# A sorted attention with a squared-ReLU feed-forward: batch 1's keys two positions per product, and the work around them reordered

## The chip, the cores and the metric

The kernel runs on one core of one Trainium2 chip. Its time is the device time of one execution in microseconds (us), a median over runs. The engines are named as in the profile: PE (TensorE: matrix products, with PEld for its weight loads), DVE (VectorE), ACT (ScalarE), POOL (GpSimd, which also issues the loads that convert fp32 to bf16) and SP (SyncE, which issues the other transfers). A name with a q behind it (SPq) is an engine's queue issuing or waiting.

## What is computed

```python
# q, k, v: (4, 8, 768, 64) fp32; sort_net: (4, 8, 8, 8); blocks of 96 positions
P = sort_net
for _ in range(5):                       # softmax-like normalisation of rows, then columns
    P = exp(P - max(P, -1)); P = P / (sum(P, -1) + 1e-9); P = P / (sum(P, -2) + 1e-9)
k_sorted = einsum('bhij,bhjcd->bhicd', P, k_blocks)      # mixes the 8 blocks
v_sorted = einsum('bhij,bhjcd->bhicd', P, v_blocks)
attn = softmax(q_block @ k_sorted_block.T / 8)            # inside each block
x = (attn @ v_sorted_block) as (3072 tokens, 512)
out = (s * relu(x @ w_in)**2 + b) @ w_out                 # w_in 512 x 2048, w_out 2048 x 512
```

## The kernel before

There are 4 batches, and each gives two token tiles of 384 tokens; tile t = 2b + half, t = 0 to 7. A token tile goes through `ffn1(t)` (16 chunks of the hidden dimension, two at a time: four products of 384 columns for each chunk, L474, then ReLU on ACT, L486, and the square on DVE, L487) and `ffn2(t)` (three groups m of 128 tokens, 16 accumulating products of 512 columns each, L498, then `store`: one DVE step, L519, that adds the bias and writes the tile `ot`, and one transfer, L522). For the last tile, `ffn2` treats its last group in parts of columns (L511).

The order on every engine is the order of the program text. The attention of the next batch is done inside the feed-forward of the present one: `ffn1` and `ffn2` take a dictionary `slots`, and call the closures of a slot between their own products. In `ffn2`, slot m*4 + f//4 follows the product f = 3, 7, 11 or 15 of group m; slot 3 thus comes at the end of group 0, behind its `store`. `halves(n)` makes the slots for batch n: `s0` for `ffn2(2(n-1))`, `s1` for `ffn2(2(n-1)+1)`.

What the closures do:

- `K` / `k_piece` (L294): sorts the keys of 16 positions with 32 products of 64 columns into one PSUM tile `tp` and moves it to `KS` with one instruction. `KP` / `k_pairs` (L304): the same with 8 products of 128 columns, two positions each, into `tpp`; four moves, two by each of DVE (L206) and ACT (L204). Before the change, batch 1 uses `K` and batches 2 and 3 use `KP`.
- `V` / `v_piece` (L330): sorts values from `VP` (a permuted copy of the values, made by ACT and POOL) into `VS`. Only batches 0 and 1 use it. For batches 2 and 3, `v_rows` (L349) sorts the values in place and `v_back` sends them through memory (`vd`) to `VS` by SP transfers.
- `SC` / `s_piece` (L381): scores of one head pair and half of the blocks; ACT then takes the exponential (L389). `P` / `p_piece` (L423): products with the values; DVE divides (L428, L429) into `x`. `TD` / `t_dma`: SP's transposing transfer of `x` into `xt`, which `ffn1` reads.
- `PDB` / `build_pd`: five small DVE steps that build the sorting matrix `PD` of a batch.
- `make_bias`: column sums of `w_out` on PE (L573), four DVE steps (L575, L578), and three POOL copies (L581) that spread the result over 128 partitions. `store` reads it.
- `load_q_rows` (L116): eight loads on POOL of one block of queries each, into `qtok`; `q_dma` (L457): two transposing transfers on SP, one for each half of the blocks, into `qt`.

PSUM is in two pools: `psa` with three buffers of two banks (tag "a": `hps`, `tp`, `tpp`, `tv`, `sc`, `pv`, `cps`, in turn), and `psb` with two buffers of one bank (tag "b": `ops` and others). A buffer is written again only when its last reader is done. `ot` has three buffers, which come free when their transfer has landed.

On POOL, batch 1's loads come in this order: values, keys, queries; then the copies of `make_bias`; then `after` (a wait for the end of `ffn1(1)`) and `v_sort` (the second part of `VP`); then batch 2's value loads, which wait for the second query transpose (L90). On SP, the two query transposes come before all stores.

Of the kernel before, what the change touches and what calls it, by code (L numbers as in the profile page):

```python
# [9 lines left out]
FP = mybir.dt.float32  # L10
BF = mybir.dt.bfloat16
# [11 lines left out]
def kernel(  # L23
# [12 lines left out]
    nc = tc.nc  # L36

    B, H, S, D = q.shape
    NB = sort_net.shape[-1]
    BLK = S // NB  # L40
    BH = B * H
    NHP = H // 2
    d_model = H * D
    d_ff = moe_w_in.shape[1]
    NF = d_ff // 128
    HB = NB // 2
    TG = HB * BLK
# [5 lines left out]
    CK = 16  # L53
# [6 lines left out]
    rawp = ctx.enter_context(tc.tile_pool(name="rawp", bufs=2))  # L60
# [9 lines left out]
    psb = ctx.enter_context(tc.tile_pool(name="psb", bufs=2, space=bass.MemoryType.PSUM))  # L70
# [9 lines left out]
    for c in range(0, C2, CV):  # L80
        nc.sync.dma_start(out=v0f[:, c:c + CV, :].rearrange("p c d -> p (c d)"),
                          in_=raw[2][0][:, c * D:(c + CV) * D])

    RAW = {}

    def load(t, b, parts=1, behind=None):
        ti = rawp.tile([128, C2, D], BF, tag=f"raw{t}", name=f"raw{t}")
        RAW[t, b] = ti
        if behind is not None:
            nc.gpsimd.tensor_copy(out=ti[0:behind.shape[0], 0, 0:1], in_=behind)  # L90
        n = C2 // parts
        for c in range(0, C2, n):
            nc.gpsimd.dma_start(out=ti[:, c:c + n, :].rearrange("p c d -> p (c d)"),  # L93
                                in_=raw["qkv".index(t)][b][:, c * D:(c + n) * D])
# [12 lines left out]

    QTOK = {}

    def load_q_rows(b):  # L110

        ti = rawp.tile([BLK, NB, H, D], BF, tag="rawq", name="qtok")
        qv = q[b].rearrange("h (n t) d -> t n h d", n=NB)
        for n in range(0, NB, 2):
            for h in range(2):
                nc.gpsimd.dma_start(out=ti[:, n + h], in_=qv[:, n + h])  # L116
        QTOK[b] = ti

    zeros = const.tile([128, 512], BF)
    nc.vector.memset(zeros, 0.0)  # L120
# [58 lines left out]
    for t, src in ((s_bc, moe_s), (b_bc, moe_b)):  # L179
        nc.gpsimd.dma_start(out=t, in_=src.to_broadcast([128, 1]))  # L180
    load("k", 1, 6)
    load_q_rows(1)

    rstat = const.tile([BH, NB], FP)
    rrec = const.tile([BH, NB], FP)
# [16 lines left out]
    def evac(eng, out, in_):  # L202
        if eng == "A":
            nc.scalar.copy(out=out, in_=in_)  # L204
        else:
            nc.vector.tensor_copy(out=out, in_=in_)  # L206

    def q_banks(b, half, engs):
# [3 lines left out]
        for u in range(2):  # L212
# [13 lines left out]
            out=jsel, in_=ident.rearrange("p (h j z) -> p j h z", h=H, j=NB), axis=AX.XY, op=ALU.add),  # L226
        lambda: nc.vector.tensor_reduce(
            out=bm.rearrange("p (e z a) -> p e z a", e=2, z=2),
            in_=idv.rearrange("p a e j z -> p e z a j"), axis=AX.X, op=ALU.add),
# [67 lines left out]
                                 start=True, stop=True)  # L297
        evac(eng, KS[b % 2][:, :, :, c0:c0 + CK], ps.rearrange("p c z g -> p g z c"))

    def k_pairs(b, c0):  # L300
        m = CK // 2
        ps = psa.tile([128, m, 2, 2 * NG], FP, tag="a", name="tpp")
        for j in range(m):
            nc.tensor.matmul(out=ps[:, j].rearrange("p e g -> p (e g)"),  # L304
                             lhsT=RAW["k", b][:, c0 + 2 * j:c0 + 2 * j + 2, :].rearrange(
                                 "p c d -> p (c d)"),
                             rhs=PD[b].rearrange("p e z g -> p (e z g)"), start=True, stop=True)
        for e in range(2):
            for u in range(2):
                evac("DA"[e],  # L310
                     KS[b % 2][e * 64:(e + 1) * 64, :, :, c0 + u:c0 + CK:2],
                     ps[u * 64:(u + 1) * 64, :, e].rearrange("p c (z g) -> p g z c", z=2))

# [38 lines left out]

    def v_back(b):
        vd = drp.tile([2, 2, NG, C2, D], BF, tag="vd", name="vd")
        nc.sync.dma_start(out=vd.rearrange("e z g c d -> (e z g) (c d)"),
                          in_=RAW["v", b].rearrange("p c d -> p (c d)"))
        for z in range(2):
            for e in range(2):
                nc.sync.dma_start(
                    out=VS[b % 2][z * GAP:z * GAP + C2, e * NG:(e + 1) * NG, 0:D],  # L360
                    in_=vd[e, z].rearrange("g c d -> c g d"))
# [116 lines left out]
    def ffn1(t, slots, done={}):  # L478

        gt = gtp.tile([128, NF, TG], BF, tag="gt", name="gt")  # L480
        GT[t] = gt
        for i in range(NF // 2):
            part(t, i, range(done.get(i, 0), NHP))
            rt = rtp.tile([128, 2, TG], BF, tag="rt", name="rt")
            h = H1.pop((t, i))[:, :, 0:TG]
            nc.scalar.activation(out=rt, in_=h, func=AF.Relu)  # L486
            nc.vector.tensor_tensor(out=gt[:, 2 * i:2 * i + 2, :], in0=rt, in1=rt, op=ALU.mult)  # L487
            for p in slots.get(i, ()):
                p()
        XT.pop(t)  # L490

    def ffn2(t, slots):
        gt = GT.pop(t)
        last = t == 2 * B - 1
        for m in range(TG // 128 - int(last)):
            ops = psb.tile([128, d_model], FP, tag="b", name="ops")
            for f in range(NF):
                nc.tensor.matmul(out=ops, lhsT=gt[:, f, m * 128:(m + 1) * 128],  # L498
                                 rhs=wo[:, f, :], start=(f == 0), stop=(f == NF - 1))
                if f % 4 == 3:  # L500
                    if f == NF - 1:
                        store(t, m, ops)
                    for p in slots.get(m * 4 + f // 4, ()):
                        p()
        if last:
            m = TG // 128 - 1
            for n0 in range(0, d_model, d_model // 2):
                ns = slice(n0, n0 + d_model // 2)
                ops = psb.tile([128, d_model // 2], FP, tag="b", name="ops")
                for f in range(NF):  # L510
                    nc.tensor.matmul(out=ops, lhsT=gt[:, f, m * 128:(m + 1) * 128],  # L511
                                     rhs=wo[:, f, ns], start=(f == 0), stop=(f == NF - 1))
                store(t, m, ops, ns)
# [3 lines left out]
    def store(t, m, ops, ns=slice(0, d_model)):  # L517
        ot = osb.tile([128, d_model], FP, tag="ot", name="ot")
        nc.vector.scalar_tensor_tensor(out=ot[:, ns], in0=ops, scalar=s_bc, in1=BIAS[0][:, ns],  # L519
                                       op0=ALU.mult, op1=ALU.add)  # L520
        r0 = t * TG + m * 128
        nc.sync.dma_start(out=out[r0:r0 + 128, ns], in_=ot[:, ns])  # L522
# [46 lines left out]
    def make_bias():  # L569
        cps = psa.tile([128, d_model], FP, tag="a", name="cps")  # L570
        for f in range(NF):
            r = slice(f % 4 * 32, f % 4 * 32 + 32)
            nc.tensor.matmul(out=cps[r], lhsT=ones, rhs=wo[:, f, :],  # L573
                             start=(f < 4), stop=(f >= NF - 4), tile_position=(0, f % 4 * 32))
        nc.vector.tensor_scalar(out=bias[0:32], in0=cps[0:32], scalar1=b_bc[0:32], scalar2=None,  # L575
                                op0=ALU.mult)
        for r in range(32, 128, 32):
            nc.vector.scalar_tensor_tensor(out=bias[0:32], in0=cps[r:r + 32], scalar=b_bc[r:r + 32],  # L578
                                           in1=bias[0:32], op0=ALU.mult, op1=ALU.add)
        for r in range(32, 128, 32):  # L580
            nc.gpsimd.tensor_copy(out=bias[r:r + 32], in_=bias[0:32])  # L581

    def QF0(): return lambda: q_banks(0, 1, "AD")
    def SB(i): return lambda: s_banks(0, 1, i)
    def K(b, i, eng): return lambda: k_piece(b, i * CK, eng)
    def KP(b, i): return lambda: k_pairs(b, i * CK)
    def V(b, i, eng): return lambda: v_piece(b, i * CK, eng)
    def SC(b, h, i): return lambda: s_piece(b, h, i)
    def P(b, h, i): return lambda: p_piece(b, h, i)
    def TP(b, h, i, eng): return lambda: t_piece(b, h, i, eng)  # L590
    def VRW(b, u): return lambda: v_rows(b, u)
    def VB(b): return lambda: v_back(b)
    def TD(b, h): return lambda: t_dma(b, h)
    def PDB(b): return lambda: build_pd(b, later[:, b % 2, b // 2, :])
# [4 lines left out]
    def halves(n):  # L599

        if n == 1:
            s0 = {4: [K(n, 0, "D"), K(n, 1, "A"), K(n, 2, "D")],
                  8: [V(n, 0, "D"), V(n, 1, "A"), V(n, 2, "D")],
                  10: [V(n, 3, "A")]}
        else:
            s0 = {0: [KP(n, 0), KP(n, 1), KP(n, 2)]}
        s1 = {0: [SC(n, 0, 0), SC(n, 0, 1)],
              3: [P(n, 0, 0), SC(n, 0, 2), SC(n, 0, 3)], 4: [P(n, 0, 1)], 5: [P(n, 0, 2)],
              6: [P(n, 0, 3), TD(n, 0), SC(n, 1, 0), SC(n, 1, 1)], 8: [P(n, 1, 0)],
              9: [P(n, 1, 1), SC(n, 1, 2), SC(n, 1, 3)], 10: [P(n, 1, 2)],  # L610
              11: [P(n, 1, 3), TD(n, 1)]}
        return s0, s1

    ffn1(0, {0: [QF0()], 2: [SB(0)], 3: [P(0, 1, 0), SB(1)], 4: [P(0, 1, 1), SB(2)],
# [5 lines left out]
    part(1, 1, (0, 1))  # L620
    part(1, 0, (2,))
    part(1, 1, (2,))
    ffn1(1, {2: [PDB(1)], 4: [make_bias], 6: [PDB(2)], 7: [PDB(3)]}, {0: 3, 1: 3})
    q_dma(1)
    for d in (0, CK):
        permute(nc.scalar, 1, RAW["v", 1], ds=slice(d, d + CK))
# [3 lines left out]
    s0, s1 = halves(1)  # L630
    ffn2(0, s0)
    ffn2(1, s1)
    for b in range(1, B):
        n = b + 1
        s0, s1, u0, u1 = {}, {}, {}, {}
        if n < B:
            load("k", n, 6, XT[2 * b + 1][:, HB - 1, NHP - 1, 0:1])
            load_q_rows(n)
            s0, s1 = halves(n)
# [38 lines left out]
```

## Time and profile before

| | |
|---|---|
| median of 3 runs | 223.43 us (222.94 to 223.51) |
| profiled execution: time, span | 223.59 us, 221.8 us |
| PE, DVE, ACT, POOL busy | 214.8, 123.3, 106.1, 70.6 us |
| granted PE clock | 1.00 |
| first-stage products L474 | 512, 87.9 us busy |
| second-stage products L498 | 350 recorded, 82.4 us busy |
| moves of the keys: `tp`, DVE / ACT | 1216 ns / 1012 ns each |
| moves of the keys: `tpp`, DVE / ACT | 728 ns / 725 ns each |
| output transfers, 256 KB / 128 KB | 2.5 us / 1.7 us to landing (median) |

The span runs from the first to the last instruction; the execution's time holds some more around it. The chain of waits follows the work back from the last instruction, at each step to what released it; a line of it gives the start, the length and what ran. Some matmul records are missing from a trace, which shows as a count that is too low and a small gap called "issue". A group's line gives the line number, the engine, the operation, out<-in, the shape and the count, then the busy time and mean of one, then the idle time of the engine just before.

### The profile page before, as it was taken

The page shows a single profiled execution, that of the slowest core. Times are in us where ns is not written, and L with a number is a line of the kernel's source. Part 1 is how long each engine was busy: PE and PEld are TensorE (multiplying, and loading weights), DVE is VectorE, ACT ScalarE, POOL GpSimd, SP SyncE. Part 2 cuts the span into 40 slices and gives each one's busy share as a digit, 9 for nine tenths or more (in the row PEclk, how much of TensorE's full clock was granted, in tenths as well). Part 3 has the DMA queues.
Part 4 walks back from the last instruction along what each step waited for, and adds up shares of the span by engine and source line. Part 5 has one row for each costly group of instructions (what it writes and reads, how often), then busy time and mean ns, then how long its engine had stood idle before and what let it go on. Part 6 is the DMA issues. An engine that isn't in the chain of part 4 may idle for free.

```text
span 221.8 us, 5257 instructions
## 1 busy us (share of the span) xinstructions
PE 214.8 (97%) x2212; PEld 129.6 (58%) x2231; DVE 123.3 (56%) x251; ACT 106.1 (48%) x144; POOL 70.6 (32%) x127
## 2 busy tenths in 40 slices
PE   7999999999999999999999999999999999999993
PEld 5977766555655555666446555655446556654453
DVE  6767457549754767546616677548417744442121
ACT  4677687656144344664622535665424355650000
POOL 7659791669914004930032008800000000000000
PEclk9999999999999999999999999999999999999999
DMA  6999999999999632999999546999911440001212
GB/s 154 280 165 126 125 162 207 204 177 117 116 182 165 183 96 46 138 236 127 91 252 171 138 121 91 236 147 92 221 69 50 121 120 0 0 3 47 95 47 95
DMA packets 66935, 28.92 MB, mean 130 GB/s; under 512 B 51808, under 2 KB 62816, under 8 KB 66912
## 3 DMA queue, kind: packets, MB, share of 16 engines
q0 software_dynamic: 31168, 12.85, 49.6%
q1 hardware_dynamic: 35744, 15.74, 34.3%
q8 instruction: 17, 0.28, 0.6%
q14 instruction: 6, 0.05, 0.1%
HBM read 28.85 MB, written 7.86 MB: 165 GB/s over the span
## 4 chain that ended last, share of the span: by engine, by line
PE 95%; DVE 2%; issue 1%; ACT 0%
PE hps L474 38%; PE ops L498 36%; PE z L132 5%; PE pv L423 4%; PE sc L381 3%; PE ops L511 2%; PE tv L330 2%; PE tp L294 1%; PE tpp L304 1%; PE tvr L349 1%; DVE vs L206 1%; PE tr L440 1%; PE scb L399 1%; PE sc L259 0%; PE pv L417 0%
## 5 line engine op out<-in xcount | busy, mean ns | idle before, releaser
L474 PE MATMUL hps<-xt,wi 128*128 128x384 bf16 x512 | 87.9, 326 | 0.0
L498 PE MATMUL ops<-wo,gt 128*128 128x512 bf16 x350 | 82.4, 379 | 1.5 <-issue 0.8
L486 ACT ACTIVATE rt<-hps 128x768 bf16<-128x768 f32 x64 | 51.8, 811 | 39.5 <-PE hps L474 38.8
L474 PEld LDWEIGHTS <-wi 128*128 128x128 bf16 x512 | 49.0, 98 | 32.6 <-issue 0.4
L487 DVE TENSOR_TENSOR gt<-rt 128x768 bf16<-128x768 bf16 x64 | 35.6, 558 | 41.2 <-ACT rt L486 41.0
L498 PEld LDWEIGHTS <-gt 128*128 128x128 bf16 x368 | 34.0, 98 | 37.2
L519 DVE SCALAR_TENSOR_TENSOR ot<-ops,s_bc,bias 128x512 f32<-128x512 f32 (+1 forms) x25 | 18.2, 729 | 37.9 <-PE ops L498 34.4
L389 ACT ACTIVATE at<-sc 112x768 bf16<-112x768 f32 x24 | 18.1, 808 | 31.8 <-PE sc L381 31.8
L429 DVE TENSOR_TENSOR x<-pv,rec 96x512 bf16<-96x512 f32 x32 | 22.0, 687 | 1.1
L116 POOL DMA_DIRECT2D qtok<-in_q_dram x24 | 18.6, 810 | 0.7 <-DMA rawk<-in_k_dram 0.6
L423 PEld LDWEIGHTS <-at 112*128 112x128 bf16 (+1 forms) x256 | 12.9, 101 | 6.7 <-ACT at L389 1.0
L142 POOL DMA_DIRECT2D wi<-in_moe_w_in_dram x24 | 13.0, 583 | 6.0 <-DMA qh<-in_q_dram 3.1
L423 PE MATMUL pv<-vs,at 112*128 112x66 bf16 (+1 forms) x256 | 13.9, 195 | 0.1
L93 POOL DMA_DIRECT2D rawk<-in_k_dram x21 | 11.2, 551 | 4.3 <-DMA rawv<-in_v_dram 2.0
L132 PE MATMUL z<-zeros 128*64 128x96 bf16 (+2 forms) x129 | 10.8, 257 | 1.3 <-DVE zeros L120 1.2
L93 POOL DMA_DIRECT2D rawv<-in_v_dram x18 | 9.7, 555 | 5.5 <-DMA wo<-in_moe_w_out_dram 4.7
L204 ACT CAST ks<-tpp 64x512 bf16<-64x512 f32 x12 | 8.7, 725 | 4.4 <-DVE ks L206 4.1
L132 PEld LDWEIGHTS <-zeros 128*64 128x64 bf16 (+1 forms) x130 | 8.5, 128 | 3.0 <-DVE zeros L120 1.2
L90 POOL COPY rawk<-xt 128x1 bf16<-128x1 bf16 x2 | 0.4, 190 | 31.1 <-DMA xt<-x 31.1
L428 DVE RECIPROCAL rec<-pv 96x8 f32<-96x8 f32 x32 | 6.4, 200 | 6.4 <-PE pv L423 6.4
L206 DVE CAST ks<-tpp 64x512 bf16<-64x512 f32 x12 | 8.7, 728 | 0.2
L351 DVE CAST rawv<-tvr 128x512 bf16<-128x512 f32 x12 | 8.2, 683 | 0.0
(93 smaller groups left out, 141.6 us busy)
## 6 DMA issues: line engine op xcount, KB each, us to landing
out_dram<-ot SPq DMA_DIRECT2D x23, 256.0 KB, 2.5
rawv<-in_v_dram POOLq DMA_DIRECT2D x18, 128.0 KB, 5.1
rawk<-in_k_dram POOLq DMA_DIRECT2D x18, 128.0 KB, 4.5
qtok<-in_q_dram POOLq DMA_DIRECT2D x24, 96.0 KB, 6.7
wo<-in_moe_w_out_dram POOLq DMA_DIRECT2D x4, 512.0 KB, 10.4
v0f<-in_v_dram SPq DMA_DIRECT2D x4, 384.0 KB, 7.1
vd<-rawv SPq DMA_DIRECT2D x2, 768.0 KB, 6.8
vs<-vd SPq DMA_DIRECT2D x8, 192.0 KB, 7.4
```

The lines of the kernel that those rows point to most:

```text
L93: nc.gpsimd.dma_start(out=ti[:, c:c + n, :].rearrange("p c d -> p (c d)"), in_=raw["qkv".index(t)][b][:, c * D:(c + n) * D])
L116: nc.gpsimd.dma_start(out=ti[:, n + h], in_=qv[:, n + h])
L132: nc.tensor.matmul(out=z[0:m, 0:w], lhsT=zeros[:, 0:m], rhs=zeros[:, 0:w], start=True, stop=True)
L142: nc.gpsimd.dma_start(out=wi[:, al, f0:f1], in_=wiv[:, al, f0:f1])
L389: nc.scalar.activation(out=at, in_=sc[0:KR, :, 0:TG], func=AF.Exp, scale=scale)
L423: nc.tensor.matmul(out=pv[0:m, e, n * VW:(n + 1) * VW], lhsT=atf[:, c0:c0 + m], rhs=VS[b % 2][:, e * NG + g0 + n, :], start=True, stop=True)
L429: nc.vector.tensor_tensor(out=x[:, :, hp * 128:(hp + 1) * 128].rearrange("p n (e d) -> p e n d", e=2), in0=pvv[:, :, :, 0:D], in1=rec.unsq ...
L474: nc.tensor.matmul(out=H1[t, i][:, f, 0:TG], lhsT=wi[:, hp, fc:fc + 128], rhs=XT[t][:, :, hp, :], start=(hp == 0), stop=(hp == NHP - 1))
L486: nc.scalar.activation(out=rt, in_=h, func=AF.Relu)
L487: nc.vector.tensor_tensor(out=gt[:, 2 * i:2 * i + 2, :], in0=rt, in1=rt, op=ALU.mult)
L498: nc.tensor.matmul(out=ops, lhsT=gt[:, f, m * 128:(m + 1) * 128], rhs=wo[:, f, :], start=(f == 0), stop=(f == NF - 1))
L519: nc.vector.scalar_tensor_tensor(out=ot[:, ns], in0=ops, scalar=s_bc, in1=BIAS[0][:, ns], op0=ALU.mult, op1=ALU.add)
```

## The change

- Batch 1's keys are sorted by `k_pairs` in slot 3 of `ffn2(0)`, where `k_piece` did it in slot 4. `k_pairs` takes the order of the engines; for batch 1 ACT moves the first half of the partitions and DVE the second, for the others it stays DVE, then ACT.
- Batch 1's values: three tiles in slot 9 (were in slot 8), the fourth in slot 0 of `ffn2(1)` ahead of the scores (was in slot 10 of `ffn2(0)`).
- `load_q_rows` takes the blocks to load, in the same order as before. For batch 1 the last three blocks are loaded at the end of `make_bias`, behind its POOL copies.
- The `PD` of batches 2 and 3 is built in slot 1 of `ffn2(1)` and `ffn2(3)`; it was built in slots 6 and 7 of `ffn1(1)`.
- `v_back` writes `vd` in two halves of 64 partitions, and reads back the first half first.
- In the last token tile, the second group's output is stored in two halves of the columns, and the third group is computed and stored in parts of 256, 128 and 128 columns (were 256 and 256).

```diff
-    def load_q_rows(b):
-        ti = rawp.tile([BLK, NB, H, D], BF, tag="rawq", name="qtok")
+    def load_q_rows(b, ns=range(NB)):
+        if b not in QTOK:
+            QTOK[b] = rawp.tile([BLK, NB, H, D], BF, tag="rawq", name="qtok")
         qv = q[b].rearrange("h (n t) d -> t n h d", n=NB)
-        for n in range(0, NB, 2):
-            for h in range(2):
-                nc.gpsimd.dma_start(out=ti[:, n + h], in_=qv[:, n + h])
-        QTOK[b] = ti
+        for n in ns:
+            nc.gpsimd.dma_start(out=QTOK[b][:, n], in_=qv[:, n])
...
-    load_q_rows(1)
+    load_q_rows(1, range(NB - 3))
...
-    def k_pairs(b, c0):
+    def k_pairs(b, c0, engs):
...
-                evac("DA"[e],
+                evac(engs[e],
...
-        nc.sync.dma_start(out=vd.rearrange("e z g c d -> (e z g) (c d)"),
-                          in_=RAW["v", b].rearrange("p c d -> p (c d)"))
-        for z in range(2):
-            for e in range(2):
+        for e in range(2):
+            nc.sync.dma_start(out=vd[e].rearrange("z g c d -> (z g) (c d)"),
+                              in_=RAW["v", b][e * 64:(e + 1) * 64].rearrange("p c d -> p (c d)"))
+        for e in range(2):
+            for z in range(2):
...
-                    if f == NF - 1:
+                    if f == NF - 1 and last and m == TG // 128 - 2:
+                        for n0 in range(0, d_model, d_model // 2):
+                            ns = slice(n0, n0 + d_model // 2)
+                            store(t, m, ops[:, ns], ns)
+                    elif f == NF - 1:
...
-            for n0 in range(0, d_model, d_model // 2):
-                ns = slice(n0, n0 + d_model // 2)
-                ops = psb.tile([128, d_model // 2], FP, tag="b", name="ops")
+            for n0, w in ((0, 256), (256, 128), (384, 128)):
+                ns = slice(n0, n0 + w)
+                ops = psb.tile([128, w], FP, tag="b", name="ops")
...
         for r in range(32, 128, 32):
             nc.gpsimd.tensor_copy(out=bias[r:r + 32], in_=bias[0:32])
+        load_q_rows(1, range(NB - 3, NB))
...
-            s0 = {4: [K(n, 0, "D"), K(n, 1, "A"), K(n, 2, "D")],
-                  8: [V(n, 0, "D"), V(n, 1, "A"), V(n, 2, "D")],
-                  10: [V(n, 3, "A")]}
+            s0 = {3: [KP(n, 0, "AD"), KP(n, 1, "AD"), KP(n, 2, "AD")],
+                  9: [V(n, 0, "D"), V(n, 1, "A"), V(n, 2, "D")]}
...
+        if n == 1:
+            s1[0] = [V(n, 3, "A")] + s1[0]
+        if n + 1 < B:
+            s1[1] = [PDB(n + 1)]
...
-    ffn1(1, {2: [PDB(1)], 4: [make_bias], 6: [PDB(2)], 7: [PDB(3)]}, {0: 3, 1: 3})
+    ffn1(1, {2: [PDB(1)], 4: [make_bias]}, {0: 3, 1: 3})
```

More of the change, by code (lines that the diff above doesn't have):

```diff
@@ L585, in K, with KP @@
     def K(b, i, eng): return lambda: k_piece(b, i * CK, eng)
-    def KP(b, i): return lambda: k_pairs(b, i * CK)
+    def KP(b, i, engs="DA"): return lambda: k_pairs(b, i * CK, engs)
     def V(b, i, eng): return lambda: v_piece(b, i * CK, eng)
```

## The prediction

> **What bounds the kernel now.** I read the page's busy times first, then the chain of waits in order of time, then the timelines of the engines around the changed places.
>
> ```profile
> PE 214.8 (97%) x2212; PEld 129.6 (58%) x2231; DVE 123.3 (56%) x251; ACT 106.1 (48%) x144; POOL 70.6 (32%) x127
> ```
>
> PE is busy 97% of the span. The chain, cut to the places that the change touches (start, length, what):
>
> ```profile
> 50.53 4.26 PE ops L498 x19
> 54.80 1.64 PE tp L294 x96
> 56.44 0.16 issue
> 56.60 3.40 PE ops L498 x15
> 60.00 1.64 PE tv L330 x96
> ...
> 63.47 0.62 PE tv L330 x32
> 64.09 1.83 PE ops L498 x8
> 65.93 0.45 PE sc L381 x16
> ...
> 102.75 1.34 PE tpp L304 x24
> 104.09 4.96 PE ops L498 x23
> ...
> 214.91 3.51 PE ops L511 x32
> 218.42 0.03 issue
> 218.44 0.48 DVE ot L519
> ```
>
> From 20.9 us on every piece of the chain is PE. Its "issue" gaps are mostly missing records (L498 has 368 weight loads, but 350 matmuls): a `ops` product takes 4.96 / 23 = 0.216 us, and 0.16 + 0.05 is one of them. So PE never waits there. Only two things can shorten the time: fewer PE cycles, or a shorter end behind the last product. Everything else can only cost, by making PE wait.
>
> **The change part by part.** (1) *Batch 1's keys in pairs.* Removed: 96 products of 64 columns. By instruction starts, 50.53 to 59.93 holds 35 `ops` products (7.55 us), the keys, and a gap of 0.095 us before the values: the keys cost 9.39 - 7.55 - 0.095 = 1.75 us (1.64 in the chain, and a like gap before them). Added: 24 products of 128 columns, as batch 2's at 102.75, 1.34 us with no gap on either side. Saving 0.41 us; 0.31 if the gap stays.
>
> A rule speaks against this: the Trainium skill, "TensorE: Matmul & The Clock Gate", section "Back-to-back issue gap", gives about 81 ns for each 128-column product in a stream where each has its own weight load. By that 24 products would take an estimated 1.94 us, 0.2 us more than now, and the 32 products of part (6) 2.6 us instead of 1.75. This trace has just such a stream, L304, at 1.34 / 24 = 56 ns, so the measurement decides.
>
> The price is in the moves out of PSUM (lines L206 and L204, busy and mean ns):
>
> ```profile
> L206 DVE CAST ks<-tpp 64x512 bf16<-64x512 f32 x12 | 8.7, 728 | 0.2
> L206 DVE CAST ks<-tp 128x1024 bf16<-128x1024 f32 x3 | 3.6, 1216 | 0.3 <-PE tp L294 0.3
> ```
>
> Before, DVE had two moves of 1.22 us and ACT one of 1.01; now each has six of 0.73, 4.4 us. In batch 2 the second engine starts on a tile when the first has done both its moves (DVE 103.24 to 107.70, ACT 104.79 to 109.25). Here ACT goes first: its two `vp` copies end at 51.23 + 2.97 = 54.20, the first tile is done at about 54.6, so ACT works 54.6 to 59.1. DVE first has the store of tile 0, now held only by the bias (part 2) to 55.3 + 0.75 = 56.05, then moves to 60.5. The products start at 53.99 (slot 3), after the last key chunk landed at 52.1. The values follow at 53.99 + 1.34 + 24 x 0.216 = 60.5; their third tile needs the third key tile's buffer at 61.6. Slack 1.1 us, so I cost the moves at nothing; each us beyond it would be a us of PE.
>
> (2) *Bias copies ahead of three query loads* on POOL:
>
> ```profile
> 49.50 6.16 POOL L116 DMA_DIRECT2D qtok<-in_q_dram  x8
> 55.65 1.93 POOL L581 COPY bias<-bias 32x512 f32<-32x512 f32 x3
> 57.77 3.24 POOL L198 COPY vp<-rawv 128x384 bf16<-128x384 bf16 x4
> 65.57 0.19 POOL L90 COPY rawv<-qt 128x1 bf16<-128x1 bf16 x1 [4.57 <-DMA qt<-qtok]
> ```
>
> Five loads of 0.77 end at 53.36; DVE's bias sums ended at 52.2; so the copies run 53.36 to 55.29, and the store that waited 1.2 us for them comes 2.3 us sooner. The last three loads end at 57.6 instead of 55.65; the `vp` copies stay at 57.8. Behind the last load (landed 60.89) stands SP's second transpose, and behind that the stores:
>
> ```profile
> 55.46 6.89 SPq L457 DMA_TRANSPOSE qt<-qtok  x2
> 62.40 7.82 SPq L522 DMA_DIRECT2D out_dram<-ot  x4
> ```
>
> The shift is between 0 (the DMA engines were busy throughout, and do the same work) and 1.95 us (the issue's whole delay); I take 1. The first store lands at 66.15 + 1 = 67.1 (68.1 at worst); its `ot` buffer, one of three, is wanted at 68.5: nothing. The second transpose lands at 66.5 (67.5), wanted at about 72.6: nothing. Batch 2's value loads, released by it, land at 74.5 (75.4) instead of 73.5, and now overlap the `xt` transpose at 73.6. That took 3.5 us; the query transpose amid loads took 6.4, the one after them 4.6, so it lands between 77.1 and 79.0, wanted at 79.0. Nothing, at the edge.
>
> (3) *Two `build_pd` moved* out of `ffn1(1)`: 1.25 us of DVE each. They now run after the stores at 65.10 and 113.62, ahead of 3.25 us of idle DVE each. Nothing; without that idle time they would delay `x` and so PE.
>
> (4) *Values at slot 9, the fourth tile with the scores.* PE work is the same. One interruption of the `ops` stream goes: alone the fourth tile costs 0.09 + 0.63 = 0.72 us (32 of the 96 cost 0.55) and the two scores 0.11 + 0.45 = 0.56, together 1.28; in one block 1.09 to 1.17. Bounds: 0 to 0.19 saved; I take 0.15, since the score blocks behind `pv` show no gap. ACT evacuates the tile in 1.02 us ahead of the exponentials, which then end at 67.3 and 68.1; the first `pv` comes at 68.6. Slack 1.3 us.
>
> (5) *`v_back` in halves.* The whole write took 90.77 to 98.18, the reads' issue until 106.9, the first query transpose lands at 112.22, the scores start at 114.38, now 113.8. Halved, the first reads can go at 94.5 to 98.2. Hidden either way: no gain. Bound for the loss: if each half takes the whole 7.41 us, the third read goes at 105.6 instead of 99.6, and PE waits 6.0 - 1.6 = 4.4 us. I take nothing: 768 KB in 7.41 us is 104 GB/s, beside the key and query loads, and two halves hold the same bytes.
>
> The Trainium skill, "SBUF — State Buffer", section "Can I just issue two DMAs to hit both halves?", says that such halves run one after the other, at little over the rate of one. With its 196 GB/s for 64 partitions that is an estimated 4 us for both, so the rule would give no loss here either.
>
> (6) *Last outputs.* The store of tile 1 becomes two of 0.48, done at 215.9 before the next at 216.66. The last tile is 256 + 128 + 128 columns: 32 products at 55.8 for 16 at 109.5 ns, 0.035 us more. The last DVE step shrinks: 512 columns took 0.75, 256 took 0.48, so 128 take 0.35: 0.13 saved. The last transfer: 256 KB took 2.0 us, 128 KB 1.7; 64 KB take 1.55 to 1.7; I take 0.1 saved. Then SP's closing waits. SP's transfers use eight semaphores in turn; before, the last of 52 fell on the fourth, and after its landing at 220.66 four waits of 0.06 us for the others followed. With four more transfers (two in `v_back`, one in each of the split stores) the last falls on the eighth, and those waits are over before it lands: 0.24 saved, or 0 if the order changes.
>
> Sum: 0.41 + 0.15 - 0.035 + 0.13 + 0.1 + 0.24 = 1.0 us. The profiled execution took 223.59 us, 1.79 beyond its span of 221.8, and 0.16 above the median of 223.43. So: span 220.8, profiled 222.6, median 222.4.
>
> **Rivals.** (A) *Only the products count*: the closing waits keep their order, the fourth value tile saves nothing, or the `xt` transpose costs PE about 0.5 us. Then the gain is 0.4 to 0.6: about 222.9. For it: the semaphore order is inferred, and the transpose is at the edge. Against: the eight semaphores do go round without a break in this trace. (B) *Slower: the halved write holds the queries back.* Place: SP's third read of batch 2, at 99.6 us, with the query transposes queued behind it. It decides from the second half landing later than 99.6 + 1.6 = 101.2 us, 10.4 after its issue; at the bound PE waits 4.4 us: 223.43 - 1.0 + 4.4 = 226.8. At half that wait it is 224.6. Against: 104 GB/s beside other loads is no limit of this write alone. (C) *The pairs don't save*: PE waits at slot 9 for the third key tile, because the moves run longer beside POOL's copies. 1.5 us beyond the slack of 1.1 cancels all: 223.4 to 223.9. Against: the 24 moves in batches 2 and 3 all took about 0.73.
>
> **How the numbers follow.** A change of 0.3%, 0.67 us, is about what a measurement of this kernel can tell from none. Forecast 0.67 (222.0 to 222.75), A 0.17, C 0.08, B 0.08. Faster by more than that is the forecast's share, 0.67; A and most of C lie within, 0.24; B and C's worst are slower, 0.09. The range's low end is the sum with every upper value (0.41 + 0.19 - 0.035 + 0.13 + 0.15 + 0.24 = 1.09, 222.3) less 0.3 for the runs' own spread (222.94 to 223.51); its high end takes in A with a small stall, 223.2.
>
> **What would show it.** In the changed profile: `tpp` x24 in 1.34 us near 54 us; no PE idle time before L330, L423 and L474 between 54 and 82 us; the last DVE `ot` at about 0.35 us; the last landing within 0.1 us of SP's last wait; span near 220.8. Wrong: a wait of PE for ks moves near 61 us, for `xt` near 79, or for `qt` near 114.

## The result and the profile after

The changed kernel takes 222.70 us (222.26 to 222.91), the kernel before 223.41 (222.94 to 225.46) beside it: a ratio of 0.9961, 95% interval 0.9950 to 0.9971. By the ratio that is 0.87 us less (0.65 to 1.12); the medians differ by 0.71 us, the means by 0.85. The forecast was 222.4, the range 222.0 to 223.2.

The profiled execution took 222.54 us, its span is 220.4. First the page's busy times and the chain of waits at the same places as before (start, length, what); line numbers have moved by a few, L497 is L498, L302 is L304, L328 is L330, L380 is L381, L514 is L511 and L522 is L519.

```profile
PE 213.6 (97%) x2156; PEld 128.8 (58%) x2175; DVE 126.0 (57%) x257; ACT 109.4 (50%) x149; POOL 70.8 (32%) x127
```

```profile
50.12 3.40 PE ops L497 x15
53.52 1.34 PE tpp L302 x24
54.86 2.16 PE ops L497 x10
57.02 0.05 issue
57.08 2.97 PE ops L497 x13
60.04 1.64 PE tv L328 x96
61.68 0.16 issue
61.84 2.54 PE ops L497 x11
64.38 0.62 PE tv L328 x32
65.00 0.45 PE sc L380 x16
...
213.99 3.55 PE ops L514 x48
217.54 0.03 issue
217.56 0.35 DVE ot L522
```

The keys' 24 products take 1.34 us, 56 ns each, as batch 2's did; the fourth value tile stands directly ahead of the scores; from 53 to 79 us no piece is a wait of PE. The last DVE step is 0.35 us long.

To compare two executions I count from the first product of the bias (line L573 before), because the stage ahead of it, which the change leaves alone, ended at 44.96 to 45.43 us in the profiled executions of this study, whatever the kernel. The two profiled executions differ thus:

| stretch, us | before | after | difference |
|---|---|---|---|
| start to the first bias product | 45.43 | 45.02 | -0.41 (not the change's) |
| to the first `pv` product of batch 1 | 23.477 | 22.967 | -0.510 |
| from there to the last DVE step | 149.536 | 149.580 | +0.044 |
| last DVE step | 0.484 | 0.351 | -0.133 |
| last transfer, issue to landing | 1.706 | 1.555 | -0.151 |
| landing to the end of the span | 1.159 | 0.918 | -0.241 |

Without the first row the sum is -0.99 us; the forecast's sum was -1.0.

Not all of this arrives in the time, which is longer than the span by a part that no trace here shows. For the kernel before, that part was 1.72 to 1.84 us (85 executions beside the experiments, median 1.77); for the changed kernel it was 2.09 to 2.22 (22 executions, median 2.13). So 0.36 us of what the span gained is lost outside it. The part goes with the kernel more than with the execution: about 1.8 us in the kernels below with only the last outputs, with four more transfers, with only the keys in pairs and with DVE first, 2.0 with the sorted values written whole, 1.7 to 2.1 with the fourth tile in pairs, and 2.1 in the others. Its cause stays open. Where it differs between two kernels, their spans tell more than their times; the median span is 220.6 us for the changed kernel and 221.6 to 221.7 for the kernel before.

The three timelines of the changed places (start, length, engine, line, what). POOL:

```profile
48.19 3.87 POOL L115 DMA_DIRECT2D qtok<-in_q_dram  x5
52.04 2.17 POOL L584 COPY bias<-bias 32x512 f32<-32x512 f32 x3
54.17 2.29 POOL L115 DMA_DIRECT2D qtok<-in_q_dram  x3
56.63 3.24 POOL L196 COPY vp<-rawv 128x384 bf16<-128x384 bf16 x4
```

DVE, then ACT:

```profile
54.25 0.75 DVE L522 SCALAR_TENSOR_TENSOR ot<-ops,s_bc,bias 128x512 f32<-128x512 f32 x1 [1.16 <-POOL bias L584]
55.51 4.52 DVE L204 CAST ks<-tpp 64x512 bf16<-64x512 f32 x6 [0.50 <-ACT ks L202]
60.06 0.75 DVE L522 SCALAR_TENSOR_TENSOR ot<-ops,s_bc,bias 128x512 f32<-128x512 f32 x1
60.73 2.34 DVE L204 CAST vs<-tv 112x1024 bf16<-112x1024 f32 x2
```

```profile
54.01 4.53 ACT L202 CAST ks<-tpp 64x512 bf16<-64x512 f32 x6 [0.21 <-PE tpp L302]
```

ACT moves keys from 54.0 to 58.5, DVE a tile behind to 60.03. The third value tile (60.04 + 2/3 of 1.64 = 61.1) finds its buffer free by 1.1 us, as worked out; by the starts of the products it is less, 0.84 us, as the memsets below show.

### The profile page after: what moved, and what is told of

It is laid out like the page before. It is cut to its first block, busy times and chain, and to the rows that moved or that the text cites. A ratio compares the mean times of both kernels' runs of the same rounds, so it can differ in the third digit from the quotient of the medians.

```text
span 220.4 us, 5172 instructions
## 1 busy us (share of the span) xinstructions
PE 213.6 (97%) x2156; PEld 128.8 (58%) x2175; DVE 126.0 (57%) x257; ACT 109.4 (50%) x149; POOL 70.8 (32%) x127
## 4 chain that ended last, share of the span: by engine, by line
PE 90%; DMA 5%; DVE 1%; issue 1%; POOL 1%; ACT 0%; POOLq 0%
PE hps L473 38%; PE ops L497 36%; DMA rawk<-in_k_dram 5%; PE pv L422 4%; PE sc L380 3%; PE tpp L302 2%; PE ops L514 2%; PE tv L328 2%; PE tvr L347 1%; DVE vs L204 1%; PE tr L439 1%; PE scb L398 1%; POOL rawk L93 0%; PE sc L257 0%; PE pv L416 0%
## 5 line engine op out<-in xcount | busy, mean ns | idle before, releaser
L497 PE MATMUL ops<-wo,gt 128*128 128x512 bf16 x350 | 82.4, 379 | 1.4 <-issue 0.6
L497 PEld LDWEIGHTS <-gt 128*128 128x128 bf16 x368 | 34.1, 98 | 37.4
L522 DVE SCALAR_TENSOR_TENSOR ot<-ops,s_bc,bias 128x512 f32<-128x512 f32 (+2 forms) x27 | 18.6, 691 | 34.7 <-PE ops L497 31.6
L202 ACT CAST ks<-tpp 64x512 bf16<-64x512 f32 x18 | 13.2, 731 | 4.7 <-DVE ks L204 4.1
L204 DVE CAST ks<-tpp 64x512 bf16<-64x512 f32 x18 | 13.1, 729 | 0.9 <-ACT ks L202 0.5
L130 PE MATMUL z<-zeros 128*64 128x96 bf16 (+2 forms) x129 | 9.8, 241 | 1.3 <-DVE zeros L118 1.2
L130 PEld LDWEIGHTS <-zeros 128*64 128x64 bf16 (+1 forms) x130 | 7.5, 115 | 3.0 <-DVE zeros L118 1.2
```

The costliest lines, as they stand in the source:

```text
L130: nc.tensor.matmul(out=z[0:m, 0:w], lhsT=zeros[:, 0:m], rhs=zeros[:, 0:w], start=True, stop=True)
```

## The experiments

Theory: PE's stream sets the span, and the change saves on it 0.41 us of keys and one interruption, and at the end a shorter last step, a shorter last transfer and two pairs of closing waits; the other edits save nothing themselves, but keep the longer key moves from making PE wait. Rivals: the small items are not what I take them for; or the moves were hidden anyway, and the other edits do nothing.

### Only the last outputs

```diff
 # the kernel before, and of the change only:
-            for n0 in range(0, d_model, d_model // 2):
+            for n0, w in ((0, 256), (256, 128), (384, 128)):
 # and the two halves of the second group's store
```

> The kernel before, with only the last outputs in parts. Theory (the sum of part 6): the last DVE step 0.48 to 0.35 us (-0.13), the last transfer 1.71 to 1.55 (-0.15), 0.035 us more of products, and with 54 SP transfers the last falls on the sixth semaphore, so that two closing waits of 0.06 fall away (-0.12): -0.37 us, a ratio of 0.998. Rival (the landing is a fixed cost and the closing waits keep their place): -0.1 us.

Measured: ratio 0.9977 (0.9966 to 0.9989), -0.5 us. In the profiled execution the last DVE step is 0.351 us, the landing takes 1.559, the closing 1.039 (from 1.159), and the last step begins 0.043 us later: -0.36 in sum. So the theory's terms, each within 0.01 us; the time's interval covers the sum.

### Four more transfers, nothing else

```diff
+        parts = [slice(0, 256), slice(256, 512)] if (t, m) in ((4, 0), (4, 1), (4, 2), (5, 0)) else [ns]
+        for cs in parts:
-        nc.sync.dma_start(out=out[r0:r0 + 128, ns], in_=ot[:, ns])
+            nc.sync.dma_start(out=out[r0:r0 + 128, cs], in_=ot[:, cs])
```

> The kernel before, with four stores in the middle (tiles 4 and 5) issued as two transfers each; DVE and PE work unchanged. Theory (closing waits): 56 SP transfers, the last falls on the eighth semaphore, and from the last landing to the end of the span it is 0.24 us less (0.90 instead of 1.15); nothing else moves: -0.24 us, ratio 0.999. Rival (the order of the closing waits has nothing to do with the count): 1.15 us again, and 0.

Measured: 0.917 us from the last landing to the end, PE's stretches the same to 0.002 us; ratio 0.9986 (0.9977 to 0.9996). This settles it: four more transfers make the kernel faster by themselves, by shifting on which of the eight semaphores, awaited in a fixed order, the last transfer falls. The order is visible instruction by instruction on SP: before, the wait for the last landing was followed by four more; now it is the last.

### Only the keys in pairs

```diff
-            s0 = {4: [K(n, 0, "D"), K(n, 1, "A"), K(n, 2, "D")],
+            s0 = {4: [KP(n, 0), KP(n, 1), KP(n, 2)],
```

> The kernel before, with batch 1's keys in pairs and nothing else: slot 4, DVE first, bias copies behind all query loads, values in slot 8. Theory (the pairs only pay with the rest): DVE's store waits for the bias to 57.6, its six moves run to 62.8, ACT's to about 64.2, and the third value tile, wanted at 60.6, waits for the third key tile: PE loses about 3.6 us and saves 0.41, +3.2 us, ratio 1.014. Rival (the moves are hidden anyway, the other edits do nothing): -0.4 us, ratio 0.998.

Measured: ratio 1.0100 (1.0077 to 1.0123), slower by 2.2 us. Its list of waits, and the end of the chain through the keys:

```profile
PE tv L330 <- ACT ks L204: 2.1, 3, 0.8
```

```profile
56.04 0.75 DVE ot L519
56.79 0.62 DVE ks L206
...
61.95 0.72 ACT ks L204
62.68 0.04 issue
62.72 0.69 PE tv L330 x32
```

Three value tiles wait for ACT's moves, the last until 62.7; the first score comes 2.12 us later than before, although the products save 0.41. The mechanism is the theory's. The size is 1.1 us under the expectation. POOL's query loads began at 47.95 us here and not at 49.50, so that the bias was there 1.6 us sooner, at 56.0 and not at 57.6, and PE itself was only 0.3 us sooner than in the profile that the expectation used.

### The order on POOL undone

```diff
 # the changed kernel, but:
-    load_q_rows(1, range(NB - 3))
+    load_q_rows(1)
...
-        load_q_rows(1, range(NB - 3, NB))
```

> The changed kernel, with all eight query loads of batch 1 ahead of the bias copies again. Theory: the first store comes 2.0 to 2.3 us later (from 54.3 to about 56.5), DVE's key moves end at 61.8 instead of 60.0, the third value tile is wanted at 61.1: PE waits about 0.7 us, +0.7 against the changed kernel, ratio to before about 0.999. Rival (the order on POOL is hidden): ratio 0.996 as the changed kernel.

Measured: ratio 1.0003 (0.9989 to 1.0017): all of the gain is gone, 0.9 us against the changed kernel. The median span is 221.3 us, 0.7 longer, as expected. The profiled execution shows the wait, but only 0.3 us of it, and was one of the quicker ones (223.00 us, of 222.66 to 224.32):

```profile
60.17 1.15 PE tv L328 x64
61.32 0.11 issue
61.43 0.69 PE tv L328 x32
```

DVE's key moves ended at 61.28 us. The third tile's first product would have started at 61.14; it started at 61.43.

### The bias held back

One and two POOL memsets ahead of the bias copies measure the slack directly.

```diff
 # the changed kernel, and in make_bias:
+        for _ in range(1):      # the second kernel: range(2)
+            nc.gpsimd.memset(pad, 0.0)     # a scratch tile, 128 x 1024
         for r in range(32, 128, 32):
             nc.gpsimd.tensor_copy(out=bias[r:r + 32], in_=bias[0:32])
```

> The changed kernel, with one more POOL memset (0.97 us, a scratch tile that nothing reads) ahead of the bias copies. Theory (slack of 1.1 us at the third value tile): the first store and DVE's key moves come 1 us later and end at about 61.0, the tile is wanted at 61.1: PE waits 0 to 0.3 us before the values. The last query loads come 1 us later too, so the xt transpose of batch 1, which landed 0.3 us ahead of its use, may cost up to 0.7 us at 79. Ratio to before 0.996 to 0.999. Rival (POOL's order is hidden by far): 0.996.

> The changed kernel, with two such memsets ahead of the bias copies. Theory: DVE's key moves end at about 62.0, the third value tile is wanted at 61.1: PE waits about 0.9 us there, whatever the xt transpose does; ratio to before at least 1.000. Rival: 0.996.

Measured: ratios 0.9979 (0.9963 to 0.9994) and 1.0004 (0.9985 to 1.0024). With two memsets the wait is where it was expected:

```profile
PE tv L328 <- DVE ks L204: 0.8, 1, 0.8
```

With one, the profiled execution shows none. Together with the other kernels that change DVE's start, from one profiled execution each:

| kernel | first query load | first store | DVE's key moves end | first score later by | ratio | median span |
|---|---|---|---|---|---|---|
| changed | 48.19 | 54.25 | 60.03 | 0 | 0.9961 | 220.6 |
| one memset | 47.63 | 54.48 | 60.07 | 0.00 | 0.9979 | 220.9 |
| matrices early (below) | 47.55 | 55.24 | 60.52 | 0.00 | 0.9987 | 221.0 |
| queries first | 47.78 | 56.01 | 61.28 | 0.32 | 1.0003 | 221.3 |
| two memsets | 48.78 | 56.69 | 61.97 | 0.96 | 1.0004 | 221.5 |

The last two columns are over all executions of a kernel; the time outside the span is 2.1 us in all five.

Wait and moves' end go together, with a knee between 60.5 and 61.3. Its place can be worked out. In the changed kernel the third value tile's first product starts at 61.01 us; where it has to wait for DVE (queries first, two memsets, and slot 8 below), it starts 0.14 to 0.15 us after the last move has ended. So the moves have to end by 60.87, and the slack is 0.84 us, where the sum had 1.1. Two memsets end them 1.10 us past that, of which 0.17 is the later start of that execution; the remaining 0.93 is the wait.

The ratios and the spans rise sooner than the profiled waits. The column of the first query load suggests why: over all fourteen profiled executions it began between 47.55 and 49.50 us, because POOL's key loads wait in some executions for an earlier load to land. An execution in which POOL is 1.3 us later spends the slack of the kernel with one memset, but not that of the changed kernel. With the matrices early it is not POOL's copies that hold the store (they had ended at 53.43) but DVE's own steps; these follow the bias sums, which wait for a small POOL load that landed between 47.42 and 49.05 us. No trace of a late execution of these two kernels was taken, so this is argued, not shown; the times of the kernel with one memset do fall into six of 222.47 to 222.88 and six of 223.16 to 224.32. A rival for the same time, the transposes of `x`, is in the last section; no run here tells the two apart.

### The sorting matrices early again

```diff
-    ffn1(1, {2: [PDB(1)], 4: [make_bias]}, {0: 3, 1: 3})
+    ffn1(1, {2: [PDB(1)], 4: [make_bias], 6: [PDB(2)], 7: [PDB(3)]}, {0: 3, 1: 3})
...
-        if n + 1 < B:
-            s1[1] = [PDB(n + 1)]
```

> The changed kernel, with the sorting matrices of batches 2 and 3 built in ffn1(1) again. Theory: 2.5 us more of DVE before its first store, which then starts at 55.6 instead of 54.25; the key moves end at about 60.8, the third value tile is wanted at 61.1: PE waits 0 to 0.2 us, ratio to before 0.996 to 0.997. Rival (this is what made room): 1 us, ratio 1.0005.

Measured: 0.9987 (0.9972 to 1.0002), 0.6 us slower than the changed kernel, 0.4 by the median spans, above the 0.2 expected. The profiled execution (222.59 us, one of the quickest of 222.53 to 223.60) has no wait before the values; it loses 0.13 us late, at a transpose of `x` (last section). The edit thus buys margin, as the table says; the forecast had counted it as nothing.

### DVE first, and the values in slot 8

```diff
-            s0 = {3: [KP(n, 0, "AD"), KP(n, 1, "AD"), KP(n, 2, "AD")],
+            s0 = {3: [KP(n, 0), KP(n, 1), KP(n, 2)],
 # and in another kernel:
-                  9: [V(n, 0, "D"), V(n, 1, "A"), V(n, 2, "D")]}
+                  8: [V(n, 0, "D"), V(n, 1, "A"), V(n, 2, "D")]}
```

> The changed kernel, with DVE first in batch 1's key moves as in the other batches. Theory: DVE's moves start behind its store at 55.0 and end at 59.5, ACT's follow a tile behind, 56.5 to 61.0; the third value tile is wanted at 61.1: PE waits 0 to 0.3 us, ratio to before 0.996 to 0.9975. Rival (the slack is not what I worked out): PE waits 1 us or more, ratio 1.001.

> The changed kernel, with batch 1's three value tiles in slot 8 again. Theory: the third tile is wanted at 59.35, and its buffer is free when DVE's last key move ends, 60.0: PE waits 0.7 us, ratio to before 0.999. Rival (the slot doesn't matter): 0.996.

DVE first: ratio 0.9963 (0.9949 to 0.9976), the same as the changed kernel. Two differences cancel in it. Its time outside the span is 1.8 us, like that of the kernel before, where the changed kernel has 2.1; and its five spans are 220.5 to 221.2, median 220.9, 0.3 us longer than the changed kernel's. The profiled execution, the slowest of the five (223.03 us), shows where PE waits:

```profile
60.90 0.72 ACT ks L202
61.62 0.04 issue
61.66 0.69 PE tv L328 x32
```

The first score comes 0.67 us later than in the changed kernel. So with ACT first PE saves up to that, and about 0.3 us in the median span, within the 0 to 0.3 expected; five executions are few, and the time alone doesn't show it.

Slot 8: ratio 0.9978 (0.9969 to 0.9986), 0.4 us slower than the changed kernel, 0.2 by the median spans; the profiled execution has 0.10 us of it before the scores. The expectation of 0.7 held an error of mine: slot 8 comes 20 `ops` products behind the keys, at 59.2, so its third tile is wanted at 60.2, not 59.35. Again what is lost is margin.

### The sorted values written whole

```diff
-        for e in range(2):
-            nc.sync.dma_start(out=vd[e].rearrange("z g c d -> (z g) (c d)"), ...)
+        nc.sync.dma_start(out=vd.rearrange("e z g c d -> (e z g) (c d)"), ...)
```

> The changed kernel, with the sorted values written back whole. Theory: the halves hide and gain nothing on PE; the count of SP's transfers falls to 54, so two closing waits come back, +0.12 us, ratio to before 0.9965. The first query transpose of batch 2 lands at about 112 instead of 110.3, before the scores at 113.5. Rival (the halves were what kept the queries on time): PE waits near 113.5.

Measured: 0.9964 (0.9953 to 0.9976). PE's stretches are the changed kernel's to 0.002 us; the closing takes 1.039 us instead of 0.918. The first query transpose of batch 2 lands at 110.80, with halves at 110.31, and 0.41 of the difference is the later start of this execution; the scores come at 113.5 or later. So the halves' only gain in the span is that they are two transfers more, 0.12 us; the ratio can't show it, since the time outside the span is 0.1 us shorter here.

### The fourth value tile alone, and in pairs

```diff
 # the changed kernel, the tile by itself:
+                  11: [V(n, 3, "A")]}
-            s1[0] = [V(n, 3, "A")] + s1[0]
 # in another kernel, sorted in pairs: 8 products of 128 columns, four moves
-            s1[0] = [V(n, 3, "A")] + s1[0]
+            s1[0] = [lambda: v_pairs(n, 3 * CK, "AD")] + s1[0]
```

> The changed kernel, with batch 1's fourth value tile in slot 11, by itself, instead of ahead of the scores. Theory: one more interruption of the ops stream, 0.10 us more of PE by the first pv product (22.97 to 23.07 us after the bias products begin), the rest as in the changed kernel; ratio 0.9965. Rival (the place of the tile matters to ACT and to the buffers): a wait of PE of 0.5 us or more.

> The changed kernel, with the fourth value tile of batch 1 sorted in pairs too: 8 products of 128 columns for 32 of 64, and four moves of about 0.73 us (ACT two, then DVE two) for one of 1.02. Theory: 0.15 to 0.2 us less PE; ACT's exponentials end 0.4 us later (67.8), DVE's moves at about 67.8, the first pv product is wanted at 67.85: no wait or up to 0.2 us; ratio 0.995 to 0.996. Rival (the moves again cost more than the products save): PE waits 0.5 us or more, ratio 0.998.

Alone: the first `pv` product comes at 23.073, 0.106 later, as expected; the ratio of 0.9972 (0.9953 to 0.9991) can't tell it.

In pairs, meant as an improvement, it is slower than both kernels: 1.0056 (1.0036 to 1.0076), 2.1 us above the changed one. The first score comes 0.18 us sooner, but the moves take 0.94 us here, and PE waits for the last:

```profile
64.88 0.94 ACT vs L202
65.81 0.01 issue
65.82 0.95 ACT vs L202
66.77 0.02 issue
66.80 0.95 DVE vs L204
67.75 0.01 issue
67.76 0.93 DVE vs L204
68.70 0.14 issue
68.83 0.43 PE pv L435 x8
```

That is 0.83 us more at the first `pv` than in the changed kernel. Another 1.03 us is lost at the end of the same chain:

```profile
215.82 3.50 DMA out_dram<-ot
219.32 0.03 issue
219.35 0.05 DVEq L535
219.40 0.04 issue
219.44 0.35 DVE ot L535
```

The last store's DVE step waits for one of the three `ot` buffers, whose transfer took 3.5 us instead of the 1.8 of the changed kernel. The section at the end comes back to this.

## Why the prediction was right

- **The number.** The mechanism held in the span: 1.0 us was forecast, 0.99 came. That the profiled execution was forecast to 0.1 us (222.6, it took 222.54) is luck: the stage ahead of the change ended 0.41 us sooner, and the time outside the span, which the forecast had kept at 1.79, was 0.35 longer. Only the second is the kernel's own, and with it the median came out at 222.70 and not at 222.4.
- **PE alone sets the span.** Right: 0.41 from the keys and 0.10 from the fourth value tile make the 0.510 us; the latter had been taken as 0.15, of 0 to 0.19.
- **The end.** The products +0.04, the last step -0.13, the landing -0.15 (taken as 0.1) and the closing waits -0.24, the last confirmed alone by the four extra transfers. That inference from the order of eight semaphores was a quarter of the gain.
- **The rule of 81 ns** (the Trainium skill, "TensorE: Matmul & The Clock Gate", section "Back-to-back issue gap") doesn't hold here: 24 products with a weight load each took 1.34 us, 56 ns each.
- **The moves cost nothing.** Right for the kernel as it is; but the slack is 0.84 us and not 1.1, since the sum left out the 0.14 us between the end of a move and the product behind it and placed that product 0.1 us late. What the prediction also missed is that the slack is needed: POOL's start varies by 2 us between executions, and edits that I had costed at nothing (matrices, slot 9) are worth 0.4 to 0.6 us by the ratios when undone, 0.2 to 0.4 by the spans.
- **POOL and SP.** The store came at 54.25, 3.4 us sooner than before, of which 1.3 is POOL's own earlier start. The shift of the second transpose did not show: it landed at 63.8, not at 66.5.
- **The `xt` transpose at the edge.** It landed at 78.39 where 78.70 was wanted; 77.1 to 79.0 was forecast. The number held by luck, for the reason was wrong: batch 2's value loads had landed at 72.2, before it began at 73.4. See below.
- **The rivals.** Of A, no item came but a smaller saving on the fourth value tile; what did take 0.36 us from the gain, the time outside the span, no rival had. The halved write (B) landed its second half at 97.8, 2.4 us behind the first and before the 101.2 from which it would have cost; both halves together took 7.95 us, the whole 7.41 before (106 GB/s, not 104, with KB of 1024 bytes). The wait of C is real, but only without the other edits, 2.2 us in the kernel with the keys alone, and for another reason: the moves took 0.70 to 0.73 us each there, as elsewhere, but they began late. (One us beyond the slack would have cancelled the gain, not the 1.5 that C names.)

## What to carry to other kernels

When one engine never waits, an edit to the span can save only its cycles or the tail; read the tail instruction by instruction, down to the order in which the last semaphores are awaited. An edit that swaps products for more moves needs room on the moving engines: find the wait that would come next, and measure the slack by holding one input back. A profile is one execution; where an early stage varies by 2 us, a wait that it doesn't show may still be in the median. And compare the spans beside the times: here 0.36 us went into the part that no profile shows.

## What the runs showed of the hardware

Packets of instructions run on the DMA engines beside the kernel's transfers, and an `xt` transpose with a 16 KB one in it took up to 2 us longer. The DMA answers for the time of the first `xt` transpose of batch 1, before and after:

```profile
q1 hardware_dynamic: 1718, 0.67, 65.5%
...
xt<-x SPq DMA_TRANSPOSE x1, 3.5
```

```profile
q1 hardware_dynamic: 1708, 0.66, 91.9%
q8 instruction: 1, 0.02, 1.1%
...
xt<-x SPq DMA_TRANSPOSE x1, 5.0
```

One 16 KB instruction packet lies in the second. Over all 84 `xt` transposes of the fourteen profiled executions, the 30 with such a packet 1.1 to 1.9 us behind their issue took 4.3 to 5.4 us, and the 54 others 3.4 to 3.64. Input loads don't explain it: 26 of the 30 had no packet of one in their time. No kernel was run that moves such a packet alone, so the cause is read from 84 cases without an exception.

The places of these packets go with the kernel. The ten kernels with batch 1's keys in pairs and the fourth value tile single have three of their six transposes hit; the kernel before, that with only the last outputs and that with four more transfers, which have 72 PE products more ahead of these places, and that with the fourth tile in pairs, which has 24 fewer, have none. Whose instructions a packet holds, the traces don't say.

This uses up margin. Before, the first transpose of each batch landed 1.7 to 1.8 us ahead of its use; in the changed kernel it is 0.26 to 0.32. With DVE first and with the matrices early, that of batch 3 landed too late (176.51 and 175.78 us), and from the first `pv` to the last DVE step PE took 0.13 us longer (149.71 us, 149.58 in the changed kernel).

In the kernel with the fourth tile in pairs, a packet of 1.19 us fell at 216.99 among the last output transfers, in the time of the one that took 3.5 us. That the packet is the cause there is read from one trace, together with seven times that agree (224.32 to 226.01).
